# Two weight units instead of four worked tile by tile at the start of an attention, ELU and expert kernel, with a rewritten order for its first stage

## The chip, the cores and the metric

The kernel runs on one core of one Trainium2 chip. Its time is the device time of one execution in microseconds; the figure to predict is the median of several executions. TensorE is PE in the rows (PEld its weight loads), VectorE is DVE, ScalarE is ACT, GpSimd is POOL, and SyncE (SP) starts the transfers.

## What is computed

Three parts follow each other. Chunked attention over 2 x 8 heads, 768 positions, head size 64:

```python
for c in range(nc):                       # chunks of 32, with 16 before and 8 after
    k_full = concat([mem_k, k[l_start:r_end]]); v_full = concat([mem_v, v[l_start:r_end]])
    a = softmax(q_c @ k_full.T / sqrt(64))
    out[c] = a @ v_full
```

Its output is read as x with 1536 tokens of 512 columns. Then an MLP with 2048 hidden columns, and a layer of eight experts in which each token goes to the expert with the largest gate value:

```python
h = x @ w_in
g = where(h > 0, h, exp(min(h, 0)) - 1)
x = g @ w_out
# then, with capacity per expert: out[i] = gate_w[i] * (relu(x[i] @ w1[e]) @ w2[e])
```

w_in and w_out arrive as 64-bit floats and are turned into 32-bit ones on the chip, by integer operations on their words.

## The kernel before

The tokens are worked in six tiles of 256. One tile is the output of one attention pair: two blocks of 128 rows, called u = 0 and 1. The hidden columns are worked in 16 units of 128; a unit is 512 KB of w_in and 512 KB of w_out, loaded by `load_unit`.

The first stage covers tiles 0 and 1 (with attention pairs 0 and 1, and most of pair 2), and while it runs, all 16 units arrive and are converted; later tiles find them ready. Its order is written out by hand in the string `ORDER` (line 33), one word for each operation, and `do` (line 862) emits them one after the other. Each engine works its own instructions in that order, and waits where an operand or a buffer isn't there. The words are:

- `lq`, `lk`, `lv` with pair and block: loads of q, k, v; `lu` and a number: load units up to it. They stand in SP's queue in this order.
- `sc`, `tm`, `ts`, `ex`, `to`, `di`, `fl`, `fc`, `av`, `xh`, `xl` with pair and block: scores on PE (L170), the largest value and the shift on DVE (L182, L202), exponentials on ACT (L213), sums on DVE, division (L233, on POOL, or with a star on DVE), transposes on PE (L239), copy on ACT (L244), product with v on PE (L255), and the two parts (high and low) of xt, the MLP's input, on ACT (L270) and DVE (L274).
- `ca` on ACT (L358), `cb`, `cc`, `cd` on DVE (L378, L382, L391): conversion of a unit's words, 128x1024 each. `ch`, `cl` are the high and low part of the unit's w_in (L403, L407), `dh`, `dl` those of its w_out. A star moves a high part from ACT to DVE, a plus a low part from DVE to POOL.
- `ma` and a step number: the first product (`gemm1`, L454, 24 matmuls) into a PSUM bank of the pool `ph` (two banks, tile `hp`). `mr` and `mv`: ELU, three passes on ACT (L468 to L470) and two on DVE (L474, L480). `mh`, `ml`: high and low part of the ELU's output (L484, L488). `mb`: the second product (`gemm2`, L509) into the tile's two accumulators, banks of the pool `ps` (six banks, shared with the attention).
- `pw`: one matmul of the identity with itself into a `ps` bank; nothing reads it (L867). It shows as two matmul records.

A step covers two (unit, tile) halves. With `NLEAD` = 4, steps 0 and 1 are units 0 and 1, then 2 and 3, of tile 0; steps 2 and 3 the same of tile 1; from step 4 on, a step is one unit with both tiles. In the first six steps (`NWHOLE`) the second product takes w_out unsplit, as four 32-bit matmuls (eight records of 128x512); later ones take twelve. From step 16 on (`ma16`, `ma17` are the first of tile 2) a loop over the steps continues, and then the experts follow.

## Time and profile before

| | |
|---|---|
| median of 3 runs | 551.16 us (550.6 to 554.33) |
| the profiled execution | 555.13 us |
| its span, first to last instruction | 553.4 us |
| busy: PE / DVE / ACT / POOL | 523.3 / 348.1 / 293.5 / 120.1 us |
| mean granted TensorE clock | 0.976 |

The profile is one execution on the chip. [...] The timeline gives start and length of instructions, merged where they repeat, and in brackets how long the engine stood idle before them and what ended that.

### The profile page before, as it was taken

What the parts mean: (1) busy time and instruction counts of PE and PEld (TensorE: products, weight loads), DVE (VectorE), ACT (ScalarE), POOL (GpSimd) and SP (SyncE); (2) the same over time, 40 slices, a digit from 0 to 9 for tenths busy, and PEclk for the clock granted to TensorE, in tenths of its full rate; (3) what the DMA queues carried; (4) which work ended last, traced back from release to release, by engine and by line L of the source; (5) the groups of instructions that cost most, each with busy time, mean ns of one, the idle gap of its engine ahead of it and who ended that gap; (6) DMA issues with size and microseconds to landing.
All of it is one profiled execution on the core that took longest, in us unless ns stands there. A gap on an engine that the chain in (4) does not pass through costs nothing. (4 is left out here: it accounts for less than half of the span.)

```text
span 553.4 us, 11372 instructions
## 1 busy us (share of the span) xinstructions
PE 523.3 (95%) x4500; PEld 448.5 (81%) x4500; DVE 348.1 (63%) x651; ACT 293.5 (53%) x569; POOL 120.1 (22%) x108
## 2 busy tenths in 40 slices
...
GB/s 332 403 414 186 100 186 291 266 359 135 1 20 139 110 1 191 145 114 87 2 3 153 198 247 98 188 152 335 117 127 165 360 253 140 335 297 220 31 7 26
DMA packets 34725, 95.93 MB, mean 173 GB/s; under 512 B 3424, under 2 KB 3424, under 8 KB 33888
## 3 DMA queue, kind: packets, MB, share of 16 engines
...
## 5 line engine op out<-in xcount | busy, mean ns | idle before, releaser
L454 PE MATMUL hp<-xt,un 128*128 128x256 f32 x1152 | 151.1, 288 | 0.8 <-POOL un L407 0.5
L454 PEld LDWEIGHTS hp<-xt,un 128*128 128x128 f32 x1152 | 144.8, 193 | 6.6 <-issue 2.4
L509 PE MATMUL ps<-un,gt 128*128 128x512 f32 x504 | 127.2, 401 | 1.4 <-POOL gt L488 1.3
L509 PEld LDWEIGHTS ps<-un,gt 128*128 128x128 f32 x504 | 92.7, 191 | 22.5 <-POOL gt L488 2.4
L805 PE MATMUL ps<-eu,ht 128*128 128x512 f32 x336 | 84.7, 404 | 6.2 <-ACT eu L695 3.4
L696 DVE TENSOR_TENSOR eu<-eraw,eu 128x1024 fp32r<-128x1024 f32 x65 | 77.3, 1225 | 19.7 <-ACT eu L695 19.5
L805 PEld LDWEIGHTS ps<-eu,ht 128*128 128x128 f32 x336 | 62.9, 191 | 21.5 <-issue 5.7
L488 POOL TENSOR_TENSOR gt<-th,gt 128x512 fp32r<-128x512 f32 x33 | 45.8, 1388 | 127.9 <-ACT gt L484 127.8
L474 DVE SCALAR_TENSOR_TENSOR th<-e,th 128x512 f32<-128x512 f32 x48 | 34.7, 723 | 52.0 <-ACT e L470 51.8
L695 ACT CAST eu<-eraw 128x1024 fp32r<-128x1024 f32 x65 | 65.1, 1045 | 0.7 <-ACT os L811 0.7
L484 ACT CAST gt<-th 128x512 fp32r<-128x512 f32 x42 | 26.1, 620 | 73.3 <-DVE th L480 73.3
L742 PE MATMUL hp<-xd,eu 128*128 128x256 f32 x480 | 59.0, 284 | 2.9 <-DVE eu L696 2.1
L742 PEld LDWEIGHTS hp<-xd,eu 128*128 128x128 f32 x480 | 58.1, 192 | 4.3 <-DVE eu L696 2.5
...
L468 ACT ACTIVATE e<-hp 128x512 f32<-128x512 f32 x48 | 28.9, 601 | 34.2 <-PE hp L454 32.5
L811 ACT ACTIVATE os<-ps,xg 128x512 f32<-128x512 f32 x15 | 10.3, 688 | 49.1 <-PE ps L805 26.0
L407 POOL TENSOR_TENSOR un<-raw,un 128x512 fp32r<-128x512 f32 x16 | 23.6, 1481 | 56.7 <-ACT un L403 40.5
L728 DVE SCALAR_TENSOR_TENSOR ht<-hp,ht 128x512 fp32r<-128x512 f32 x20 | 13.8, 690 | 33.4 <-ACT ht L727 33.4
L469 ACT ACTIVATE th<-e 128x512 f32<-128x512 f32 x48 | 30.4, 632 | 5.9 <-DVE junk L541 3.0
L480 DVE SCALAR_TENSOR_TENSOR th<-hp,th 128x512 f32<-128x512 f32 x42 | 29.1, 692 | 4.0 <-DVE th L474 0.5
L470 ACT ACTIVATE e<-e 128x512 f32<-128x512 f32 x48 | 30.4, 632 | 1.5
L767 PE MATMUL hq<-eu,xd 128*128 128x512 f32 x120 | 30.4, 398 | 0.3 <-PE ps L805 0.3
...
## 6 DMA issues: line engine op xcount, KB each, us to landing
...
disp<-in_blank_dram SPq DMA_DIRECT2D x12, 514.0 KB, 14.9
...
```

What stands on the lines that cost most here:

```text
L454: nc.tensor.matmul(hp[:, j, :], units[f].un[:, 0, wp, kk * P : (kk + 1) * P], xts[ti][:, xp, kk, :], start=(n == 0), stop=(n == 3 * KD - 1),)
L469: nc.scalar.activation(th, e, AF.Tanh, scale=0.5)
L470: nc.scalar.activation(e, e, AF.Exp, scale=-1.0)
L474: nc.vector.scalar_tensor_tensor(out=th, in0=e, scalar=1.0, in1=th, op0=ALU.add, op1=ALU.mult)
L480: nc.vector.scalar_tensor_tensor(out=to, in0=hv, scalar=0.0, in1=th0, op0=ALU.max, op1=ALU.subtract)
L488: eng.tensor_tensor(out=gt[:, 1, :], in0=th, in1=f32(gt[:, 0, :]), op=ALU.subtract)
L509: nc.tensor.matmul(accs[ti][bl], x, w, start=(f == 0 and n == 0), stop=(f == NF - 1 and n == len(passes) - 1),)
L695: nc.scalar.copy(un[:, 0, :], raw)
L696: lows.tensor_tensor(out=un[:, 1, :], in0=raw, in1=f32(un[:, 0, :]), op=ALU.subtract)
L742: nc.tensor.matmul(hp[:, j, :], w1p(kk, wp, f * P, P), xd[xp][:, kk, :], start=(n == 0), stop=(n == 3 * KD - 1),)
L767: nc.tensor.matmul(hp, self.xd[xp][:, kk, self.b0 * P : (self.b0 + 1) * P], w1p(kk, wp, i * 512, 512), start=(n == 0), stop=(n == 3 * KD - 1),
L805: nc.tensor.matmul(acc, hof(f, gp, j), w2p(f, wp), start=(f == 0 and n == 0), stop=(f == NFE - 1 and n == 2))
```

## The change

The number of units that are worked tile by tile falls from four to two: steps 0 and 1 are units 0 and 1 of tile 0 and of tile 1, and from step 2 on a step is one unit with both tiles. There are 16 steps as before, and the first six take w_out unsplit as before. The whole string `ORDER` is rewritten. The 11 matmuls `pw` go, 20 matmuls `pm` come (8, 5 and 3 ahead of and between the first transposes, 2 before ma0, 2 before the last transposes of pair 1); they write into the bank that the next first product is going to use, so that `gemm1` takes over a bank that may already be there.

```diff
-lq00 lk00 pw pw pw pw sc00 tm00 ts00 ex00 lu0 cb0 to00 ca0 lq01 cc0 lk01 pw pw pw pw sc01
...
+lq00 lk00 pm pm pm pm pm pm pm pm sc00 tm00 ts00 ex00 to00 lk01 lq01 sc01 tm01 lu0 ca0 ts01
...
-    NLEAD, NWHOLE = 4, 6
+    NLEAD, NWHOLE = 2, 6
...
+    hps = {}
+
+    def new_hp():
+        return ph.tile([P, 2, TT], F32, tag="h", name=nm("hp"))
+
+    def idle(s):
+
+        if s not in hps:
+            hps[s] = new_hp()
+        nc.tensor.matmul(hps[s][:, 0, :], ident, ident.unsqueeze(1).to_broadcast([P, 2, P]), start=True, stop=True)
+
     def gemm1(s):
         ft = steps[s]
-        hp = ph.tile([P, 2, TT], F32, tag="h", name=nm("hp"))
+        hp = hps.pop(s, None) or new_hp()
...
+        tops = [0]
...
-            if op == "pw":
-                wp = tps([P, 2, P])
-                nc.tensor.matmul(wp, ident, ident.unsqueeze(1).to_broadcast([P, 2, P]), start=True, stop=True)
+            if op == "pm":
+                idle(tops[0])
...
                 if op == "ma":
                     pend[s] = gemm1(s)
+                    tops[0] = s + 1
```

The first place is SP's queue, from its third transfer on. Before, units are `raw_14`, `raw_24` and `raw_37`; `kt_2` and `kt_3` are the k of block 0 and 1, `v_4` and `v_5` their v, `q_1` both blocks' q:

```order
L337 DMA raw_14_161<-in_moe_w_in_dram 128x1024
L337 DMA raw_14_161<-in_moe_w_out_dram 128x1024
L141 DMA q_1_93<-in_q_dram 128x512
L141 DMA kt_3_95<-in_k_dram 128x1024
L337 DMA raw_24_221<-in_moe_w_in_dram 128x1024
L337 DMA raw_24_221<-in_moe_w_out_dram 128x1024
L141 DMA kt_2_94<-in_k_dram 128x1024
L141 DMA q_1_93<-in_q_dram 128x512
L141 DMA v_4_96<-in_v_dram 128x1024
L337 DMA raw_37_327<-in_moe_w_in_dram 128x1024
L337 DMA raw_37_327<-in_moe_w_out_dram 128x1024
L141 DMA kt_3_95<-in_k_dram 128x1024
```

In the changed kernel the units are `raw_15` and `raw_25`:

```order
L141 DMA kt_3_95<-in_k_dram 128x1024
L141 DMA q_1_93<-in_q_dram 128x512
L337 DMA raw_15_206<-in_moe_w_in_dram 128x1024
L337 DMA raw_15_206<-in_moe_w_out_dram 128x1024
L141 DMA kt_2_94<-in_k_dram 128x1024
L141 DMA q_1_93<-in_q_dram 128x512
L337 DMA raw_25_287<-in_moe_w_in_dram 128x1024
L337 DMA raw_25_287<-in_moe_w_out_dram 128x1024
L141 DMA v_4_96<-in_v_dram 128x1024
L141 DMA kt_3_95<-in_k_dram 128x1024
L141 DMA q_1_93<-in_q_dram 128x512
L141 DMA v_5_97<-in_v_dram 128x1024
```

Block 1's k and q now come ahead of unit 0, pair 1's first k and q ahead of unit 1, and unit 2, the third raw tile, falls from this place to behind both v.

The second place is PE at the start of the MLP's steps (only one of each two equal second-product rows is shown). Before, from ma1 on; `un_53` and `un_63` are units 2 and 3, `un_35` and `un_36` units 0 and 1, `xt_32` tile 0, `xt_67` tile 1:

```order
L454 MATMUL hp_76_655<-xt_32_288,un_53_454 128x256 x12
L454 MATMUL hp_76_655<-xt_32_288,un_63_550 128x256 x12
L509 MATMUL ps_78_683<-raw_14_161,gt_73_607 128x512
L509 MATMUL ps_79_684<-raw_14_161,gt_73_607 128x512
L454 MATMUL hp_84_704<-xt_67_562,un_35_323 128x256 x12
L454 MATMUL hp_84_704<-xt_67_562,un_36_325 128x256 x12
L509 MATMUL ps_78_683<-raw_37_327,gt_82_695 128x512
L509 MATMUL ps_79_684<-raw_37_327,gt_82_695 128x512
L509 MATMUL ps_91_750<-raw_14_161,gt_87_735 128x512
L509 MATMUL ps_92_751<-raw_14_161,gt_87_735 128x512
```

In the changed kernel, from mb0 on; `un_37` and `un_30` are units 0 and 1, `un_60` unit 2, `un_76` unit 3, `xt_31` tile 0, `xt_55` tile 1:

```order
L520 MATMUL ps_68_653<-raw_15_206,gt_61_623 128x512
L520 MATMUL ps_69_654<-raw_15_206,gt_61_623 128x512
L465 MATMUL hp_51_537<-xt_55_550,un_37_389 128x256 x12
L465 MATMUL hp_51_537<-xt_55_550,un_30_308 128x256 x12
L465 MATMUL hp_75_704<-xt_31_311,un_60_620 128x256 x12
L465 MATMUL hp_75_704<-xt_55_550,un_60_620 128x256 x12
L520 MATMUL ps_77_737<-raw_15_206,gt_72_696 128x512
L520 MATMUL ps_78_738<-raw_15_206,gt_72_696 128x512
L465 MATMUL hp_79_745<-xt_31_311,un_76_731 128x256 x12
L465 MATMUL hp_79_745<-xt_55_550,un_76_731 128x256 x12
```

Units 2 and 3 of tile 0, which stood ahead of mb0, are gone from there; the second step is tile 1 of units 0 and 1, and one product (unit 2, both tiles) stands between it and its own second product (`gt_72`).

The third place is DVE between unit 3's conversion and the second ELU. Before, around the first ELU, with attention rows and second rows of a pair left out; `raw_46` is unit 3 and `raw_55` unit 4:

```order
L378 TENSOR_SCALAR raw_46_393<-raw_46_393 128x1024
L382 SCALAR_TENSOR_TENSOR raw_46_393<-raw_46_393 128x1024
L228 TENSOR_SCALAR su_62_537<-su_62_537 128x8
L229 RECIPROCAL su_62_537<-su_62_537 128x8
L233 TENSOR_TENSOR a_61_536<-a_61_536,su_62_537 128x512
L391 SCALAR_TENSOR_TENSOR raw_46_393<-raw_46_393 128x1024
L403 CAST un_63_550<-raw_46_393 128x512
L474 SCALAR_TENSOR_TENSOR th_72_602<-e_71_601,th_72_602 128x512
L480 SCALAR_TENSOR_TENSOR gt_73_607<-hp_54_460,th_72_602 128x512
L378 TENSOR_SCALAR raw_55_486<-raw_55_486 128x1024
L382 SCALAR_TENSOR_TENSOR raw_55_486<-raw_55_486 128x1024
L391 SCALAR_TENSOR_TENSOR raw_55_486<-raw_55_486 128x1024
```

In the changed kernel, from the last pass of unit 2 (`raw_38`) on; `raw_54` is unit 3, `raw_63` unit 4, `raw_64` unit 5:

```order
L391 SCALAR_TENSOR_TENSOR raw_38_392<-raw_38_392 128x1024
L485 SCALAR_TENSOR_TENSOR th_45_485<-e_44_484,th_45_485 128x512
L491 SCALAR_TENSOR_TENSOR gt_61_623<-hp_6_112,th_45_485 128x512
L274 TENSOR_TENSOR xt_55_550<-ps_56_551,xt_55_550 128x2x128
L378 TENSOR_SCALAR raw_54_547<-raw_54_547 128x1024
L274 TENSOR_TENSOR xt_55_550<-ps_58_585,xt_55_550 128x2x128
L202 TENSOR_SCALAR nm_62_635<-mx_48_523 128x8
L378 TENSOR_SCALAR raw_63_637<-raw_63_637 128x1024
L382 SCALAR_TENSOR_TENSOR raw_63_637<-raw_63_637 128x1024
L378 TENSOR_SCALAR raw_64_640<-raw_64_640 128x1024
L382 SCALAR_TENSOR_TENSOR raw_54_547<-raw_54_547 128x1024
L391 SCALAR_TENSOR_TENSOR raw_54_547<-raw_54_547 128x1024
```

Unit 3 was converted ahead of the first ELU and unit 4 behind it; now only unit 2 is done by the first ELU, and units 3, 4 and 5 stand between the first and the second one.

## Rows read from the trace of the kernel before

**Rows 1.** Table of stretches: busy us (instructions) of each engine, clock, transfers.

```profile
core 0: us, PE busy (x) PEld busy (x) DVE busy (x) ACT busy (x) POOL busy (x), PEclk, DMA share, GB/s
12.00:22.00 10.00, 7.43 (x148) 5.79 (x149) 8.44 (x15) 7.88 (x27) 4.43 (x4) 0.50 1.03 415
...
32.40:39.00 6.60, 6.60 (x107) 6.45 (x101) 5.67 (x12) 3.35 (x6) 1.30 (x1) 0.50 1.03 414
36.80:126.10 89.30, 88.52 (x670) 69.92 (x669) 79.55 (x108) 60.07 (x107) 24.21 (x16) 0.99 0.73 243
```

**Rows 2.** PE's timeline to its first product: start, us, instruction, [idle before].

```profile
1.58 3.64 PE L867 MATMUL ps<-ident 128*128 128x256 f32 x8 [1.58 <-POOL ident masks.py:199]
...
6.08 1.99 PE L867 MATMUL ps<-ident 128*128 128x256 f32 x8
10.33 0.85 PE L170 MATMUL ps<-kt,q 64*32 64x64 f32 x64 [2.25 <-DMA kt<-in_k_dram]
...
14.75 1.17 PE L170 MATMUL ps<-kt,q 64*32 64x64 f32 x64 [1.16 <-DMA q<-in_q_dram]
16.75 2.13 PE L255 MATMUL ps<-at,v 64*64 64x32 f32 x64 [0.83 <-DMA v<-in_v_dram]
...
24.34 0.39 PE L454 MATMUL hp<-xt,un 128*128 128x256 f32 x1
```

**Rows 3.** PE's timeline from pair 1's last transposes to ma17.

```profile
31.01 0.63 PE L239 MATMUL ps<-ident,a 128*128 128x128 f32 x4 [1.72 <-DVE a L233]
31.57 3.47 PE L255 MATMUL ps<-at,v 64*64 64x32 f32 x128
34.97 4.93 PE L454 MATMUL hp<-xt,un 128*128 128x256 f32 x24
...
42.91 3.45 PE L454 MATMUL hp<-xt,un 128*128 128x256 f32 x24
...
80.14 2.96 PE L509 MATMUL ps<-un,gt 128*128 128x512 f32 x12
82.93 3.03 PE L454 MATMUL hp<-xt,un 128*128 128x256 f32 x24
...
93.18 2.59 PE L509 MATMUL ps<-un,gt 128*128 128x512 f32 x10 [0.65 <-POOL gt L488]
...
110.30 1.13 PE L255 MATMUL ps<-at,v 64*64 64x32 f32 x64
...
127.94 2.90 PE L454 MATMUL hp<-xt,un 128*128 128x256 f32 x22 [0.48 <-POOL un L407]
...
139.14 5.91 PE L454 MATMUL hp<-xt,un 128*128 128x256 f32 x48
```

**Rows 4.** ACT's timeline: ca0, one block's exponentials with what follows, an ELU.

```profile
8.44 1.16 ACT L358 ACTIVATE raw<-raw 128x1024 f32<-128x1024 f32 x1 [0.18 <-DMA raw<-in_moe_w_out_dram]
...
14.37 0.33 ACT L213 ACTIVATE a<-ps,nm 128x64 f32<-128x64 f32 x1
...
16.69 1.25 ACT L403 CAST un<-raw 128x512 fp32r<-128x512 f32 x2
...
32.16 0.60 ACT L468 ACTIVATE e<-hp 128x512 f32<-128x512 f32 x1
```

**Rows 5.** DVE's timeline: unit 2 landing, and a wait for an ELU.

```profile
19.16 1.13 DVE L378 TENSOR_SCALAR raw<-raw 128x1024 int32<-128x1024 int32 x1 [1.25 <-DMA raw<-in_moe_w_out_dram]
...
41.95 0.69 DVE L474 SCALAR_TENSOR_TENSOR th<-e,th 128x512 f32<-128x512 f32 x1 [1.43 <-ACT e L470]
```

**Rows 6.** Groups by form, 0 to 140 us: busy us, mean ns | idle before.

```profile
L391 DVE SCALAR_TENSOR_TENSOR raw<-raw 128x1024 int32<-128x1024 int32 x15 | 19.8, 1318 | 0.3
L382 DVE SCALAR_TENSOR_TENSOR raw<-raw 128x1024 int32<-128x1024 int32 x15 | 18.3, 1219 | 1.0 <-DVE raw L378 0.5
...
L474 DVE SCALAR_TENSOR_TENSOR th<-e,th 128x512 f32<-128x512 f32 x17 | 13.2, 779 | 8.3 <-ACT e L470 8.3
L378 DVE TENSOR_SCALAR raw<-raw 128x1024 int32<-128x1024 int32 x15 | 12.1, 820 | 2.1 <-DMA raw<-in_moe_w_out_dram 2.1
```

More of the change, by code (lines that the diff above doesn't have):

```diff
@@ L33 @@
 ORDER = """
-lq00 lk00 pw pw pw pw sc00 tm00 ts00 ex00 lu0 cb0 to00 ca0 lq01 cc0 lk01 pw pw pw pw sc01 tm01 ts01 lu1 ca1 di00 pw fl00 cd0 fc00 cb1 cc1 cd1 ex01 to01 lk10 lq10 lv00 sc10 av00 ch0 ch1 lu2 tm10 di01 cb2 lk11 xh00 xl00 ca2 pw fl01 fc01 lv01 pw av01 lq11 ts10 cl1+ cc2 cd2 lu3 ex10 lq20 to10 lk20 xh01 xl01 lv11 sc11 tm11 ts11 ch2 ca3 cb3 cc3 cl0+ ma0 lv10 lu4 sc20 lu5 lu6 di10 fl10 cl2+ ex11 to11 di11* cd3 ch3* tm20 fl11 fc10 av10 xh10* fc11 mr0 mv0 av11 xh11 xl11 lq21 cl3+ cb4 ca4 cc4 cd4 xl10 ma1 lu7 mb0 mr1 mv1 ch4 cl4+ ca6 cb6 cc6 cd6 ma2 mr2 mv2 lu8 ts20 ch6 cl6+ lk21 mb1 mb2 ma3 lu9 cb7 cb9 cb5 ca7 dh6 dl6 ex20 ca5 lu10 ca10 cc7 cd7 ca8 mr3 cc5 cd5 dh0* mv3 sc21 ma4 dl0+ to20 di20 mb3 ch5 cl5 cb8 dh1 dl1 mr4 ca9 cc9 mv4 ch7 dh2 dl2+ cb10 cl7 ma5 cd9 mr5 dh7 cc8 mv5 mb4 dh4 lu11 tm21 ca11 cd8 dl4 lu12 ca12 cc10 ma6 mr6 mv6 ch9 dh9 dh3 dl3 mh6 dl7+ mb5 dh5* lv20 cl9+ ts21 ex21 ml6+ ch8* dh8 to21 cl8+ lu13 dl8 ma7 mr7 mv7 mb6 ma8 fl20 ma9 dl5+ cb11 mh7 mr8 cd10 ch10 cb12 ml7 mb7 dl9 mv8 mh8 ml8+ mb8 cl10 ma10 cc11 cd11 mr9 mv9 lv21 lu14 dh10 dl10+ lu15 ca15 ch11 cl11 mh9 ml9 cc12 cd12 mb9 fc20 ma11 mr10 mv10 mh10 ml10 di21 mb10 fl21 ch12 dh12 cl12 ma12 dl12 cb13 dh11 dl11 ca13 cc13 cd13 mr11 mv11 ch13 cl13 fc21 mh11 ml11 ca14 cb14 cc14 av20 xh20 xl20 dh13 dl13+ mb11 cd14 ch14* mr12 dh14 mv12 mh12 ml12 cb15 cc15 av21 xh21 ma13 mr13 mv13 mh13 cl14+ ma14 xl21 mr14 dl14+ mb12 ml13 mb13 cd15 ch15* cl15+ mv14 mh14 ma15 ml14 mb14 dh15 dl15 mr15 mv15 mh15 ml15 ma16 mr16 mv16 mh16 ml16+ mb15 ma17 mr17 mv17 mh17 ml17 lw lz0 lz1 lz2 lz3 lz4 lz5 lz6 lz7 lz8 lz9 lz10 lz11
```

1 line of the change is left out of this document (added).

## The prediction

> **What bounds the kernel now.** The page gives PE 523.3 of 553.4 us, an average over stages, so I read the stretch table next. From 36.8 to 126.1 us PE is busy 88.52 of 89.3 us and DVE 79.55 [rows 1]: PE is the bound of the two-tile stage, and DVE behind it has only 9.75 us to spare. Looser is the start. [...] PE's timeline shows what it waits for at the start: 2.25 us for k of row block 1, 1.16 for a q, 0.83 for a v [rows 2], then 1.72 for a division of pair 1 on DVE [rows 3]. From 31.01 on it has two more waits, 0.65 and 0.48, until ma17 starts at 139.14 [rows 3]. [...] Behind the stage the same instructions follow in the same order and PE is full again, so I let a shift of ma17 pass to the end.
>
> **The change part by part.**
>
> *The unbroken run.* Both orders have the same products, second products and pair work. Before, ma1 begins it at 34.97; pairs 0 and 1 and ma0 are then done. In the new order the same has been done when mb0 starts, and the same work lies ahead up to ma17. Its length is 139.14 - 34.97 = 104.17, less the waits 1.13, less what ma1 lost at 1.2 GHz, 4.93 - 3.45 = 1.48 [rows 3]: 101.6 us.
>
> *When mb0 can start: transfers.* Unit 0 has landed at 8.44 (1.75 MB asked for up to there) and unit 2 at 19.16 (5.75 MB) [rows 4, 5], so 0.373 MB a us. In the new queue this puts k and q of block 1 at 7.8, unit 0 at 10.5, k and q of pair 1 at 12.5, unit 1 at 15.1, v at 16.5, the next k and q at 18.5, v at 19.8, unit 2 at 22.5, k and q of pair 2 at 25.2, v of pair 1 at 27.9, unit 3 at 30.5, unit 4 at 33.2, unit 5 at 35.9. Units 2 and 3 are no longer ahead of pair 1's second half.
>
> *Warm-ups.* The old first four took 3.64 us and the second four 1.99 [rows 2], so eight in a row end at about 7.2, and sc00 starts there and not at 5.31. That 2 us is nearly free: fl00 must wait for the division of pair 0, behind which k of pair 1 lands at 12.5 anyway; without that cover it would cost the 2 us. The other twelve stand where PE would wait, and their bank is the next product's, so they hold no attention bank.
>
> *The chain to ma0.* sc00 to 8.1; softmax of block 0 and then of block 1 on DVE to 12.4; the eight exponentials of one block take 16.69 - 14.37 = 2.3 us [rows 4], to 14.9; DVE to 16.3; ca1 (1.16 [rows 4]) has to go before the next exponentials on ACT, which end at 19.0; fc01 to 19.6; av01 with v at 19.8, 1.1 us [rows 3], to 20.9; xt's two halves to 22.8. Unit 0's last pass on DVE, its cast and its low part on POOL come out at 22.7. ma0 starts at 22.8, against 24.34 [rows 2].
>
> *From ma0 to mb0.* ma0 ends at 25.7, sc20 at 26.5. ACT ends the last exponentials of pair 1 at 26.0, then needs three passes of 0.6 [rows 4] for the ELU, to 27.9, and two copies, to 29.1. av10 and av11 end at 30.7, and mb0 takes the bank that xl10 gives up on DVE: **31.0**. Without waits ma17 then starts at 31.0 + 101.6 = 132.6, 6.5 us earlier than 139.14.
>
> *The new wait at mb1.* Step 1 is now tile 1 of the same two units, so mb1 follows ma1 by one product only. mv1 on DVE stands behind cb4, cc4, cb5, cc3, cd3 and cd4; cb5 waits 1.3 us for unit 5; mv1 is done at 41.3 and PE is ready at 40.2: 1.1 us. Behind mb1 stands ma3, and nothing else is on PE.
>
> *DVE, the cost that comes back.* At mb0 DVE has converted units 0 to 2 and one pass of unit 3; before, at that point, four units. The passes moved cost 0.82, 1.22 and 1.32 us [rows 6]. Counted with such means, DVE's list from cb4 to ch15 before is 83.6 us; the stretch shows 79.55 [rows 1], so 0.952 of it. The new list from xl11 (done at 32.3) to cl15 is 88.1 us, so 83.9: ready at 116.2 with no gap at all. To it I add the 1.3 us for unit 5 and the idle time of before that is not a wait for an ELU. Five waits for an ELU, 4.7 of the 9.75 us, the first 1.43 at 41.95 [rows 5], vanish where DVE is the late one; 5.0 stays. That gives cl15 at 122.5. PE would want it at 132.6 + 1.1 less the tail from ma15 on, two products 5.91 and three second products of 82.93 - 80.14 = 2.79 [rows 3]: 14.3, so at 119.4. ma17 therefore starts between 133.7 (PE decides) and 122.5 + 14.3 = 136.8 (DVE decides). I take 135.5, nearer to DVE's end, because before already waited 0.48 for unit 15's low part [rows 3] with 4.3 us less in the list.
>
> *At nothing.* Low parts moved between DVE and POOL: DVE gets four more and three split parts fewer, one copy of xt goes to ACT. POOL works 24.21 of 89.3 us [rows 1]. Unit 0's w_out products read the same words. If this cover is gone, one low part costs its 0.8 us on DVE.
>
> *The clock.* The first fall, before 12.0, follows the 2.25 us wait; the second, at 32.4, the 1.72 us one [rows 1 to 3]. In my chain the longest waits are about 1.2 us before fl00 and 1 us before fl01. I take PE at 2.4 GHz from sc01 on; the other end is the first rival. [...]
>
> **The sum.** 139.14 - 135.5 = 3.6 us earlier. The profiled execution took 555.13 us (span 553.4), the median is 551.16; I subtract from the median: 547.6. Bounds: 6.5 us if no new wait arises, 2.3 if DVE decides.
>
> **The rivals.**
>
> *The clock falls in the new start too.* [...] Against: the warm-ups halve the gaps. Price: three warm-ups at the rate of the first (1.2 us more), a pair of av at 3.47 instead of 2.2 [rows 3], ma0 1.48, less 0.8 us of waits that this fills: 3.2. Gain 0.4: 550.8.
>
> *DVE becomes the bound (the other side).* The place is the cl and ml parts from unit 13 on, before ma13 to ma15. If DVE keeps all its 9.75 us of idle time (each ELU still late) and the 1.3, cl15 comes at 32.3 + 83.9 + 11.05 = 127.3 and ma17 at 141.6, 2.4 us later than before: 553.6. It decides from cl15 at 124.8 on. For it: every us of DVE goes straight to the end there. Against: a late DVE finds its ELU ready.
>
> *The shift does not pass.* If the tile loop waits for something not moved, 551.2. For it only the 15% "issue" of the chain that ended last; against it the full PE behind 126.
>
> *No new wait at all.* 551.16 - 6.5 = 544.7. For it: two places with 1 to 3 us of slack in my counts; against it: both engines at over 95%.
>
> **How the numbers follow.** Chances: the forecast (545.7 to 549.2) 0.48; clock 0.18; DVE bound 0.16; not passed 0.05; no new wait 0.13. About 1% is what a measurement of this kernel can tell from no change, so the bounds are 545.6 and 556.7. Faster: the no-wait case and the forecast's near edge, 0.13 + 0.09 = 0.22. Slower: the DVE rival with DVE later by 3.1 us more, 0.05. Within 1%: 0.73. The range, 544.5 to 553.0, reaches from the no-wait case to just under the DVE rival; the likeliest case's own is 545.7 to 549.2.
>
> **What would show it.** Right: ma0 near 22.8, mb0 near 31, granted clock 1.00 from 8 to 35, a wait of about 1 us for gt at mb1, DVE over 93% busy from 36 to 120, ma17 near 135.5. Wrong: a stretch at 0.50 before 35; mb0 after 33; PE waits for un or gt behind 100 us of more than 4 us together; a stage end that has moved with a kernel end that has not.

## The result, and the profile after

The changed kernel takes 556.36 us (median of 20 executions, 552.89 to 563.9), the kernel before in the same runs 553.03 (20 executions, 548.64 to 557.09). The ratio is 1.0065, with a 95% interval of 1.0044 to 1.0086: slower by 3.6 us, where 3.6 us faster was forecast. Two executions of the changed kernel in a slower state of the chip are left out of the ratio. It lies within the 1% that had the largest chance, but outside the range: 1.0065 of the forecast's 551.16 are 554.7, and the range ended at 553.0. The profiled execution took 559.7 us, its span is 558.0.

The table of stretches of the changed kernel (length of the stretch, busy us and instructions of each engine, granted clock, DMA share, GB/s):

```profile
core 0: us, PE busy (x) PEld busy (x) DVE busy (x) ACT busy (x) POOL busy (x), PEclk, DMA share, GB/s
12.00:22.00 10.00, 5.51 (x194) 4.34 (x194) 8.89 (x15) 8.11 (x39) 2.52 (x3) 1.00 1.00 393
22.00:32.40 10.40, 8.49 (x136) 7.77 (x137) 4.59 (x13) 4.81 (x22) 5.28 (x4) 0.67 0.68 245
32.40:39.00 6.60, 4.75 (x203) 4.19 (x179) 4.80 (x8) 3.91 (x8) 1.29 (x1) 1.00 1.02 414
36.80:126.10 89.30, 83.83 (x622) 65.12 (x623) 83.58 (x107) 59.26 (x105) 24.65 (x15) 0.96 0.71 236
```

The same table of the kernel before, for the one stretch that [rows 1] leave out:

```profile
22.00:32.40 10.40, 8.29 (x276) 7.17 (x278) 9.04 (x17) 7.87 (x37) 2.32 (x2) 0.99 1.02 397
```

Before, DVE worked 9.04 and 5.67 us of the two stretches from 22.0 to 39.0; now 4.59 and 4.80. It lost 5.3 us there, and the transfers fell to 245 GB/s. From 36.8 to 126.1 the places are exchanged against [rows 1]: PE 83.83 instead of 88.52 us, DVE 83.58 instead of 79.55.

PE's timeline of the changed kernel, from the scores of pair 1's second block (L170) to ma18; L465 is the first product (L454 before), L520 the second (L509 before), L456 the warm-ups:

```profile
20.07 0.86 PE L170 MATMUL ps<-kt,q 64*32 64x64 f32 x52 [0.72 <-DMA q<-in_q_dram]
23.91 0.46 PE L170 MATMUL ps<-kt,q 64*32 64x64 f32 x12 [2.98 <-issue]
24.29 1.93 PE L255 MATMUL ps<-at,v 64*64 64x32 f32 x64
26.15 2.07 PE L456 MATMUL hp<-ident 128*128 128x256 f32 x4
27.66 4.55 PE L465 MATMUL hp<-xt,un 128*128 128x256 f32 x24
...
34.82 1.29 PE L255 MATMUL ps<-at,v 64*64 64x32 f32 x73
37.96 1.01 PE L255 MATMUL ps<-at,v 64*64 64x32 f32 x55 [1.85 <-issue]
38.91 3.86 PE L520 MATMUL ps<-raw,gt 128*128 128x512 f32 x8
...
49.37 3.86 PE L520 MATMUL ps<-raw,gt 128*128 128x512 f32 x8 [0.85 <-DVE gt L491]
...
70.98 5.48 PE L520 MATMUL ps<-raw,gt 128*128 128x512 f32 x8 [1.94 <-DVE gt L491]
...
119.09 4.60 PE L465 MATMUL hp<-xt,un 128*128 128x256 f32 x24 [1.47 <-DVE th L491]
...
144.53 5.91 PE L465 MATMUL hp<-xt,un 128*128 128x256 f32 x48
151.24 3.13 PE L465 MATMUL hp<-xt,un 128*128 128x256 f32 x24 [0.79 <-DVE th L491]
```

ma0 starts at 27.66 (forecast 22.8), mb0 at 38.91 (31.0), ma17, the second half of the line at 144.53, at 147.4 (135.5; before 139.14, [rows 3]). Two waits of the start have no releaser: 2.98 us in the middle of sc11 and 1.85 in the middle of av11. Behind the waits of 2.98, 1.94 and 1.47 us the next work runs slowly: av01 1.93 instead of the 1.14 us of av00, ma0 4.55 instead of about 2.9, mb4 5.48 instead of 3.86, ma13 4.60 instead of 3.1; the granted clock is 0.50 from 23.8, 71.6 and 119.4 us on. Behind the 1.85 us in av11 it stays at 1.00.

DVE's and POOL's timelines of the changed kernel from mb2 to mb4 (L391 a conversion pass, L485 and L491 the ELU's two passes, L407 a low part):

```profile
58.20 1.23 DVE L391 SCALAR_TENSOR_TENSOR raw<-raw 128x1024 int32<-128x1024 int32 x1
59.35 1.82 DVE L485 SCALAR_TENSOR_TENSOR th<-e,th 128x512 f32<-128x512 f32 x1
61.27 0.69 DVE L491 SCALAR_TENSOR_TENSOR gt<-hp,th 128x512 f32<-128x512 f32 x1
...
66.08 2.34 DVE L391 SCALAR_TENSOR_TENSOR raw<-raw 128x1024 int32<-128x1024 int32 x1
68.35 1.79 DVE L485 SCALAR_TENSOR_TENSOR th<-e,th 128x512 f32<-128x512 f32 x1
70.24 0.69 DVE L491 SCALAR_TENSOR_TENSOR gt<-hp,th 128x512 f32<-128x512 f32 x1
```

```profile
59.13 1.49 POOL L407 TENSOR_TENSOR un<-raw,un 128x512 fp32r<-128x512 f32 x1 [4.98 <-ACT un L403]
65.22 4.37 POOL L407 TENSOR_TENSOR un<-raw,un 128x512 fp32r<-128x512 f32 x2 [4.60 <-ACT un L403]
```

DVE never idles here, and mv4's second pass ends late for mb4. The same pass takes 0.69 us alone and 1.8 beside a POOL pass, the conversion pass 1.23 and 2.34. Added up over the DVE passes beside a POOL pass (time over the shortest of the same form) this is 11 to 12 us between 48 and 140 us, with 18 POOL passes; in the kernel before, between 36 and 128, 7 to 9 us with 17. The figure hangs a little on how much overlap is counted.

### The profile page after: what moved, and what is told of

It is laid out like the page before. It is cut to its first block, busy times and chain, and to the rows that moved or that the text cites. A ratio compares the mean times of both kernels' runs of the same rounds, so it can differ in the third digit from the quotient of the medians.

```text
span 558.0 us, 11410 instructions
## 1 busy us (share of the span) xinstructions
PE 525.0 (94%) x4518; PEld 450.8 (81%) x4518; DVE 350.4 (63%) x650; ACT 293.8 (53%) x571; POOL 119.2 (21%) x107
## 5 line engine op out<-in xcount | busy, mean ns | idle before, releaser
L465 PE MATMUL hp<-xt,un 128*128 128x256 f32 x1152 | 151.7, 289 | 2.3 <-DVE th L491 2.3
L465 PEld LDWEIGHTS hp<-xt,un 128*128 128x128 f32 x1152 | 145.5, 194 | 8.2 <-issue 4.4
L520 PE MATMUL ps<-un,gt 128*128 128x512 f32 x504 | 126.5, 400 | 0.8 <-POOL gt L499 0.6
L520 PEld LDWEIGHTS ps<-un,gt 128*128 128x128 f32 x504 | 92.8, 190 | 21.4 <-POOL gt L499 1.1
L816 PE MATMUL ps<-eu,ht 128*128 128x512 f32 x336 | 82.9, 398 | 3.2 <-ACT eu L706 2.4
L499 POOL TENSOR_TENSOR gt<-th,gt 128x512 fp32r<-128x512 f32 x36 | 50.4, 1400 | 154.0 <-ACT gt L495 153.9
L816 PEld LDWEIGHTS ps<-eu,ht 128*128 128x128 f32 x336 | 61.8, 188 | 17.7 <-issue 2.4
L485 DVE SCALAR_TENSOR_TENSOR th<-e,th 128x512 f32<-128x512 f32 x48 | 37.3, 777 | 54.2 <-ACT e L481 54.0
L407 POOL TENSOR_TENSOR un<-raw,un 128x512 fp32r<-128x512 f32 x13 | 21.2, 1637 | 51.9 <-ACT un L403 51.9
L491 DVE SCALAR_TENSOR_TENSOR th<-hp,th 128x512 f32<-128x512 f32 x42 | 29.0, 692 | 3.7
```

The source lines that it names most:

```text
L465: nc.tensor.matmul(hp[:, j, :], units[f].un[:, 0, wp, kk * P : (kk + 1) * P], xts[ti][:, xp, kk, :], start=(n == 0), stop=(n == 3 * KD - 1),)
L485: nc.vector.scalar_tensor_tensor(out=th, in0=e, scalar=1.0, in1=th, op0=ALU.add, op1=ALU.mult)
L491: nc.vector.scalar_tensor_tensor(out=to, in0=hv, scalar=0.0, in1=th0, op0=ALU.max, op1=ALU.subtract)
L499: eng.tensor_tensor(out=gt[:, 1, :], in0=th, in1=f32(gt[:, 0, :]), op=ALU.subtract)
L520: nc.tensor.matmul(accs[ti][bl], x, w, start=(f == 0 and n == 0), stop=(f == NF - 1 and n == len(passes) - 1),)
L816: nc.tensor.matmul(acc, hof(f, gp, j), w2p(f, wp), start=(f == 0 and n == 0), stop=(f == NFE - 1 and n == 2))
```

## The experiments

Four theories: **A**, the start (TensorE runs out of instructions, the clock falls, all is late); **B**, DVE's list decides from mb0 on, with **P**, POOL's help costs DVE about what it saves; **C**, the warm-ups pay; **E**, the step list. Stage lengths are read from mb1's start to mv17's second pass on DVE, which leaves the start out: 105.1 us in the changed kernel (49.37 to 154.49).

**The step list alone.** In the kernel before:

```diff
-    NLEAD, NWHOLE = 4, 6
+    NLEAD, NWHOLE = 2, 6
```

> The kernel before with the new step list alone (two units tile by tile instead of four); the order of work is that of before. Theory A (in the changed kernel TensorE runs out of instructions in its start: 2.98 us of 'issue' inside sc11 and 1.85 inside av11, the clock falls, and everything behind is late): the list costs nothing, ma17 at 139 to 140 and a time within 0.3% of before. Theory B (DVE's list between mb0 and cl15 is too long): same list as before, so also within 0.3%. Theory E (the step list itself costs, since mb1 now follows its own product at once): a wait of 1 to 3 us at mb1, repeated, and a time 2 to 4 us above before, ratio 1.004 to 1.008.

557.04 us, ratio 1.0067 (1.0038 to 1.0096). This looks like E, but PE's timeline names something else:

```profile
41.39 5.28 PE L454 MATMUL hp<-xt,un 128*128 128x256 f32 x23 [4.35 <-DVE xt L274]
```

ma1 is now tile 1's product and stands 4.35 us for xl10, which DVE makes behind unit 4's conversion, and runs slowly after it. That is the place of a word, not the list; so the list alone, with xl10 moved:

```diff
-xh11 xl11 lq21 cl3+ cb4 ca4 cc4 cd4 xl10 ma1
+xh11 xl11 xl10 lq21 cl3+ cb4 ca4 cc4 cd4 ma1
```

> The kernel before with two lead units, and with the low part of pair 1's first half (xl10) ahead of unit 4's conversion on DVE. In the run with the list alone ma1 stood 4.35 us for that part, which DVE made behind unit 4, since ma1 now takes tile 1; that wait is no property of the list. Theory B (the list is harmless, the changed kernel loses by its longer and later DVE work): ma1 waits under 0.7 us, ma17 at 138 to 140, time within 0.3% of before. Theory E (the list itself costs, by a second product right behind its first and units asked for earlier): ma17 at 142 or later, time 2 to 4 us above before.

551.89 us, ratio 1.0012 (0.9979 to 1.0045). With xl10 in its place the list costs nothing that can be measured; E falls. ma1 waited 1.07 us for it, a little more than expected.

**The place of the wait for instructions.**

```diff
-lq00 lk00 pm pm pm pm pm pm pm pm sc00
+lq00 lk00 pm pm pm pm pm pm pm pm pm pm pm pm pm pm sc00
```

> The changed kernel with six more warm-ups ahead of its first eight, which puts 12 more matmuls in front of everything. Theory A: instructions come in pieces of a fixed count, so the place of the 2.98 us wait is counted from the program's first instruction: it comes 12 matmuls earlier, after 40 of sc11's 64 matmuls instead of 52, and the 1.85 us one after about 61 of av10 and av11's 128 instead of 73. If the wait were for data of sc11, or an accident of that place, it would stay behind 52 matmuls (rival D: something on SP's queue) or vanish. Time: 0 to 3 us more than the changed kernel under every theory.

562.55 us, one execution. The wait in sc11 was not there at all; the one in av11 came after 61 matmuls, as A said:

```profile
32.03 1.12 PE L255 MATMUL ps<-at,v 64*64 64x32 f32 x61
35.30 1.80 PE L255 MATMUL ps<-at,v 64*64 64x32 f32 x67 [2.14 <-issue]
```

**The changed kernel again**, to see which of its waits belong to it:

> The changed kernel once more, nothing edited. In its first profile ma0 started at 27.66, behind 2.98 us of 'issue' inside sc11, and mb0 at 38.91; in three edited kernels whose start is nearly the same that wait was absent and ma0 started at 24.2 to 26.1. Theory A (the wait inside sc11 is part of the change's cost): it is there again, ma0 after 27. Theory B (it belonged to that one execution; DVE's list decides): no such wait, ma0 at 24.0 to 24.8, mb0 at 34.5 to 37 with the 1.5 to 2.2 us wait inside av11 still there, TensorE waits for DVE again at mb1 (0.85), mb4 (1.9), ma13 (1.5), and ma17 about 108 us behind mb0, so at 143 to 145.

560.16 us: the wait in sc11 is back with 3.31 us, the one in av11 has 2.03, mb1, mb4 and ma13 wait 0.85, 1.94 and 1.47, mb0 stands at 37.65 and ma17 at 147.8. So both profiles of this kernel have all of these waits. The one in sc11 is missing in e2, and further down in e3, e4 and e13, whose PE does the same work up to there: it comes and goes between executions.

**Less under way ahead of the instructions.**

```diff
-ch0 lv01 lu2 xl00 av01 xh01 xl01 ts11 cb2 lq21 ca2 cl0+ to10 cc2 ex11 to11 lk20 lq20 pm pm ma0 mr0
+ch0 lv01 xl00 av01 xh01 xl01 ts11 lq21 lu2 cl0+ to10 ex11 to11 lk20 lq20 pm pm ma0 cb2 ca2 cc2 mr0
```

> The changed kernel with unit 2's load moved behind the load of q that waits for sc11 (and its three conversion steps behind ma0), so that about 1 MB less is under way between 15 and 22 us. Theory A (the piece of instructions asked for at 14.8 us stands behind the loads issued before it, and came at 21.7 when they had drained): the piece comes near 19.5, the wait inside sc11 shrinks from 2.98 to under 1 us, ma0 starts at 24.5 to 25.5 instead of 27.66, the low clock near 24 us is gone or shorter, ma17 at 143 to 145 instead of 147.4, time 2 to 4 us under the changed kernel, that is within 0.3% of before. Theory B: ma0 earlier, but ma17 stays near 147 and the time that of the changed kernel (ratio to before 1.005 to 1.008). If the wait in sc11 keeps its 3 us although nothing is ahead of the piece, A's reason for the lateness is wrong.

558.22 us, ratio 1.0057 (1.0023 to 1.0090). The packet of instructions that sc11 waits for (see the next section) started at 17.7 instead of 21.6, the wait in sc11 was gone and ma0 stood at 24.65. But mb0 came at 36.68 only, behind 2.21 us in av11, and ran slowly (5.48 us); mb1 and mb4 waited 0.85 and 1.98 as before, and mv17 came at 153.93. The start was 2.7 to 3.0 us better at ma0, 0.6 to 1.0 at mb1, and the time was not: this is B's outcome, though with so little left at mb1 it is a weak test of A. It doesn't show that the later load took the wait away, since e2, e4 and e13 lacked it without that.

**DVE with less to do.** cd left out for units 6 to 13:

```diff
-            for lw, hw in zip(self.lows(), self.highs()):
+            for lw, hw in () if 6 <= self.f <= 13 else zip(self.lows(), self.highs()):
```

> The changed kernel without the conversion's last pass (the sign bits, 1.2 us on DVE each) for units 6 to 13: about 10 us of DVE's work between 49 and 120 us are left out, so it computes with wrong signs of those weights and its time is one with less work. Theory B (DVE decides from mb0 on): the waits of TensorE at mb4 (1.94), ma13 (1.47) and ma18 (0.79) and the low clock behind them (about 3 us) go, ma17 at 140 to 142 instead of 147.4, time 5 to 7 us under the changed kernel. Theory A alone (only the start matters): ma17 at 145 to 147, the two waits at the start stay at 3.0 and 1.9, time 0 to 2 us under the changed kernel.

537.87 us, ratio 0.9737 (0.9694 to 0.9779). Other signs send other tokens to other experts, so the whole time can't be compared; up to mv17 the work is the same. mb1 to mv17 took 98.0 us instead of 105.1. Of PE's waits over 0.2 us only mb1's own and ma18's are left:

```profile
45.23 3.86 PE L520 MATMUL ps<-raw,gt 128*128 128x512 f32 x8 [0.85 <-DVE gt L491]
...
140.01 3.14 PE L465 MATMUL hp<-xt,un 128*128 128x256 f32 x24 [0.79 <-DVE th L491]
```

10 us less on DVE gave 7.1: DVE decides in this stretch.

**ELU passes earlier in the list.** In the changed kernel mb4 waited 1.94 us for mv4 and ma13 1.47 for mv11, and each then ran slowly at a granted clock of 0.50 (5.48 us instead of 3.86, 4.60 instead of 3.1):

```diff
-ma5 dh2 dl2 cc9 ca7 cc7 ca11 cd9 mr4 mv4 mb4
+ma5 mr4 mv4 dh2 dl2 cc9 ca7 cc7 ca11 cd9 mb4
-fl21 fc21 cc13 cd13 ch13 dh11* dl11 ml10+ mb10 mv11
+mv11 fl21 fc21 cc13 cd13 ch13 dh11* dl11 ml10+ mb10
```

> The changed kernel with two pairs of ELU passes on DVE moved up: mv4 ahead of the conversion steps dl2, cc9, cc7, cd9, and mv11 ahead of cc13, cd13, dh11, dl11. [...] Theory B' (only the places are wrong, DVE has enough time): both waits and both slow products go, ma17 about 102 to 103 us behind mb0 instead of 107.3 to 108.5, and the time 3.5 to 6 us under the changed kernel, ratio to before 0.995 to 1.001. Theory B (the length of DVE's list decides): the waits come back at later products (mb6 to mb12, or ma14 to ma16), ma17 105 us or more behind mb0, time 0 to 2.5 us under the changed kernel.

558.18 us, ratio 1.0071 (1.0042 to 1.0100). mb4 no longer waited; mb5 did, and longer:

```profile
76.87 5.44 PE L520 MATMUL ps<-raw,gt 128*128 128x512 f32 x8 [3.36 <-DVE gt L491]
```

mb1 to mv17 took 104.9 us. A place in the list moves the wait on; its length is what costs.

Both edits (unit 2 later, ELU passes earlier):

> The changed kernel with both edits, unit 2's load behind the q that waits for sc11 and the two ELU passes earlier. Theory B': mb0 at 36 to 37 as with unit 2 later alone, ma17 102 to 103 us behind it, near 139, time at or under before (ratio 0.993 to 1.001). Theory B: ma17 105 us or more behind mb0, near 142, ratio 1.000 to 1.005.

558.17 us, ratio 1.0070 (1.0034 to 1.0107), 104.9 us from mb1 to mv17, 3.35 us at mb5: the same again.

**More work for POOL.** Nine low parts get a plus (the words alone; what stands between them is left out here and in the next two cuts):

```diff
-dl1 dl2 dl4 dl5 dl7 dl8 dl10 dl11 dl12
+dl1+ dl2+ dl4+ dl5+ dl7+ dl8+ dl10+ dl11+ dl12+
```

> The changed kernel with nine low parts of w_out (dl1, dl2, dl4, dl5, dl7, dl8, dl10, dl11, dl12; 0.8 us each on DVE) given to POOL, which works under a third of that stretch: same work, 7.2 us less on DVE. Theory B (DVE decides from mb0 on): TensorE's waits at mb4 (1.94) and ma13 (1.47) shrink to under 1 us together, ma17 comes 103 to 106 us behind mb0 instead of 108.5, and the time is 2.5 to 5 us under the changed kernel, at or below before (ratio 0.996 to 1.002). Theory A (only the start counts): ma17 still 108 us behind mb0 and a ratio of 1.004 to 1.009. If POOL becomes late in DVE's place, TensorE waits for un or gt from POOL instead.

575.17 us, ratio 1.0411 (1.0351 to 1.0471). mb4 waited 1.98 us although two of DVE's parts ahead of it were gone, and mb6 waited 13.64 us for ml6, which stands behind dl10 in POOL's order: POOL's order became the bound, as the last sentence feared, so only the unchanged mb4 says something on P.

**No help from POOL.** Fifteen low parts lose their plus:

```diff
-cl4+ dl0+ cl6+ dl3+ dl6+ cl9+ ml6+ dl9+ cl11+ ml9+ cl12+ ml10+ cl13+ ml12+ ml14+
+cl4 dl0 cl6 dl3 dl6 cl9 ml6 dl9 cl11 ml9 cl12 ml10 cl13 ml12 ml14
```

> The changed kernel with the fifteen low parts that POOL makes between mb1 and ma16 (cl4, dl0, cl6, dl3, dl6, cl9, ml6, dl9, cl11, ml9, cl12, ml10, cl13, ml12, ml14) given to DVE, 0.69 us each, 10.4 us in all. In the trace DVE's passes beside a POOL pass take up to 1.1 us longer (11.2 us in all between 48 and 140 us, of 87.7 busy). Theory P (POOL's work costs DVE about as much as doing it): the longer passes go, DVE's list grows by less than 3 us, ma17 105 to 110 us behind mb0, time within 3 us of the changed kernel. Theory B without P (DVE decides and POOL's help is real): ma17 114 us or more behind mb0, time 6 to 10 us above the changed kernel, ratio to before 1.017 or more.

569.30 us, ratio 1.0253 (1.0215 to 1.0292). Here too the order broke in one place: ml6 had been written late because POOL made it, and on DVE it stood behind all the passes ahead of it in the list, which DVE worked through without a gap from 84.9 to 97.9 us. DVE's and PE's timelines:

```profile
59.95 0.68 DVE L485 SCALAR_TENSOR_TENSOR th<-e,th 128x512 f32<-128x512 f32 x1
...
67.01 1.22 DVE L391 SCALAR_TENSOR_TENSOR raw<-raw 128x1024 int32<-128x1024 int32 x1
68.14 0.68 DVE L485 SCALAR_TENSOR_TENSOR th<-e,th 128x512 f32<-128x512 f32 x1
```

```profile
98.64 7.32 PE L520 MATMUL ps<-un,gt 128*128 128x512 f32 x22 [12.42 <-DVE gt L499]
```

Up to there P is seen plainly: the passes that took 1.82, 2.34 and 1.79 us take 0.68, 1.22 and 0.68, and mv8 comes 40.8 us behind mb1 instead of 44.8, with five more parts on DVE. The sum beside POOL fell from 11 to 12 us to 0.85.

**Only the five parts ahead of that place.**

```diff
-cl4+ dl0+ cl6+ dl3+ dl6+
+cl4 dl0 cl6 dl3 dl6
```

> The changed kernel with only the first five of POOL's low parts (cl4, dl0, cl6, dl3, dl6, between mb1 and mb5) given to DVE; everything behind keeps its place. Theory P (a POOL pass costs DVE about 1.1 us here, a low part on DVE itself 0.69): mv4 and mv5 come 1.5 to 2.5 us earlier behind mb1 than in the changed kernel (20.9 and 26.3 us), the wait at mb4 (1.94) and the slow product behind it go, mv17 101 to 103 us behind mb1 instead of 105.1, time 2 to 4 us under the changed kernel. Theory B without P: 3.4 us more work for DVE, the wait at mb4 grows to 3 us or more, time 1 to 3 us above the changed kernel.

552.90 us against 552.90 of the kernel before, ratio 1.0015 (0.9984 to 1.0046). PE's timeline at mb4:

```profile
66.33 3.87 PE L520 MATMUL ps<-raw,gt 128*128 128x512 f32 x8 [0.23 <-DVE gt L491]
69.61 3.46 PE L465 MATMUL hp<-xt,un 128*128 128x256 f32 x24
```

The wait fell from 1.94 to 0.23 us, the slow product went, mb1 to mv17 took 101.9 us. mv4 and mv5 came 19.2 and 24.9 us behind mb1, 1.7 and 1.4 earlier. DVE had 3.4 us more of its own to do, and was earlier all the same. P holds, and it is worth most of what the change lost: 3.5 us between the medians, 2.8 by the ratios.

**The warm-ups.** All 20 are taken out:

```diff
-lq00 lk00 pm pm pm pm pm pm pm pm sc00
+lq00 lk00 sc00
...
-di00 pm pm pm pm pm fl00
+di00 fl00
...
```

> The changed kernel without its 20 warm-ups (their bank goes to the product alone). [...] Theory A (they only spend instructions and push sc00 from 5 to 7.5 us): 36 matmuls fewer before ma0, so the wait of 'issue' moves from behind the 52nd matmul of sc11 to behind the 20th of av01 or goes, and the one in av11 moves behind the 109th; sc00 near 5.3, mb0 1 to 3 us earlier. Theory B: whatever the start does, mb1 still waits 0.85 and mb4 1.9 for DVE, and the time changes by less than 2 us.

560.26 us, ratio 1.0106 (1.0060 to 1.0151), so not faster. sc00 started at 5.06, ma0 at 24.62 and mb0 at 36.68, the waits for instructions moved as A said (after 19 matmuls of av01, 2.24 us; after 113 of av10 and av11, 2.12), and mv17 came at 152.76. Up to there the matmuls ran slowly: the scores took 1.17 us instead of 0.86, ma0 5.00. The start gained 1 to 2 us against the changed kernel's two profiles and mb1 none (49.75). The profile has one more wait of 2.50 us for instructions in the experts. Whether the warm-ups are worth something stays open: the difference to the changed kernel is inside the two intervals.

**Moving the pieces by 48 pairs.** Two ways were tried, and neither left the rest of the start as it was: first 32 warm-ups of 64 columns for the first eight (e14; e15 with the five parts on DVE), then 48 of a score's size for two of them (e16, with the five parts; reckoned as 46 pairs more than in e13, 552.90 us).

```diff
+            nc.tensor.matmul(hps[s][:, 0, 0:n], ident, ident[:, 0:n], start=True, stop=True)
```

```diff
+            nc.tensor.matmul(
+                hps[s][0:CH, 0, 0:n], ident[0:64, 0:CH], ident[0:64, 0:n], start=True, stop=True, tile_position=(0, 0)
+            )
```

> The changed kernel with its first eight warm-ups cut into 32 of a quarter of the width: the same columns and bank, but 48 more instruction pairs ahead of everything. Theory A (instructions come in pieces of 128 pairs of weight load and matmul; TensorE runs dry where it goes through one faster than the next one lands): the piece that began behind 73 of av10 and av11's matmuls now begins behind about 25, and the one before it at ma0's start instead of inside sc20, which gives it 6 us instead of 5; the 1.5 to 2.8 us wait inside av11 shrinks under 0.7 us or goes, and with it the slow mb0; mb0 1 to 3 us earlier, at 33.5 to 35.5. If the wait stays at the 73rd matmul of av10 and av11, the count has nothing to do with it. Time: 0 to 3 us under the changed kernel; theory B holds the gain to less than that, since mb4 still waits for DVE.

> Both edits. If the two causes are those of the miss, they add: mb0 at 33.5 to 35.5, no wait over 1 us behind mb1 but ma13's, ma17 at 138 to 141 (before: 139.1; changed kernel: 147.4 and 147.8), and a time of 5 to 7 us under the changed kernel, ratio to before 0.995 to 1.001. If the time does not follow ma17, the rest lies behind 155 us.

> [...] Theory A: the piece that began behind 73 of av10 and av11's 128 matmuls begins behind about 29; asked for at ma0's start and not inside sc20, it lands in time, the 1.95 us wait goes, mb0 at 33.5 to 34.5 instead of 35.97 and the time 1 to 2 us under the same kernel without it. Against A: the wait moves to about the 29th matmul and keeps its 1.5 to 2.5 us; time within 1 us.

561.57, 558.25 and 563.49 us, ratios 1.0176 (1.0136 to 1.0217), 1.0121 (1.0085 to 1.0156) and 1.0197 (1.0160 to 1.0234). PE's first line in e14 and in e16, and the wait in av10 and av11 of e14 and of e16:

```profile
1.58 13.92 PE L457 MATMUL hp<-ident 128*128 128x64 f32 x64 [1.58 <-POOL ident masks.py:199]
```

```profile
1.58 10.44 PE L457 MATMUL hp<-ident 64*32 64x64 f32 x96 [1.58 <-POOL ident masks.py:199]
```

```profile
39.44 0.59 PE L255 MATMUL ps<-at,v 64*64 64x32 f32 x25
42.50 1.72 PE L255 MATMUL ps<-at,v 64*64 64x32 f32 x103 [2.47 <-issue]
```

```profile
45.89 0.54 PE L255 MATMUL ps<-at,v 64*64 64x32 f32 x19 [1.68 <-issue]
```

A quarter of the columns took more than half the time (0.22 us a record against 0.39), and the small matmuls into one place 0.11 us a record, two records each, not the 0.012 of a score; so the first scores came 7.7 to 9.2 us late and none of the three shows what the wait is worth. They show its place: e14's stands after 25 matmuls, where A put it (e15 had none there), and e16's, with 92 records more in front and not the 46 reckoned, after 109. And they repeat e13: with the five parts the same start is 3.3 us faster (561.57 to 558.25), though e15's profile also lacks the wait in av10 that e14's has, so not all of it need be theirs.

**What helped, together.** Five parts on DVE, unit 2 later, mv11 earlier:

> The changed kernel with five of POOL's low parts on DVE, unit 2's load behind the q that waits for sc11, and mv11 ahead of cc13, cd13, dh11 and dl11. Each took a wait away where it was tried (2.98 inside sc11, 1.47 at ma13). Theory B with P (DVE decides, POOL lengthens it): DVE has 0 to 2 us to spare now, so ma13's wait shrinks to 0.5 to 1 and the time is 0 to 2 us under the kernel with five parts alone, ratio to before 0.997 to 1.002. If only the start counted (A), 2 us or more less: 0.995 to 0.998.

554.00 us, ratio 1.0028 (0.9998 to 1.0057): no gain over the five parts alone. ma13 waited 0.95 us for POOL's cl13 instead, and the wait in sc11 was there (1.98) in spite of the later load, so the load's place is not what decides it.

**Does a shift pass to the end?** In the kernel before, 22 matmuls of the warm-ups' form stand in ma17's bank ahead of ma17, so that TensorE alone works longer there; 9.5 us were reckoned, about what the changed kernel's mv17 is late, and its profile shows 9.66:

```diff
+        for _ in range(22 if s == 17 else 0):
+            nc.tensor.matmul(hp[:, 0, :], ident, ident.unsqueeze(1).to_broadcast([P, 2, P]), start=True, stop=True)
```

> [...] If a shift there passes to the end as the forecast let it: time 8.5 to 10 us above before, ratio 1.015 to 1.018. If later stages give part of it back: 3 to 6 us, ratio 1.005 to 1.011, and the changed kernel's 3.3 us are what is left of its 9.5.

```profile
137.28 9.66 PE L451 MATMUL hp<-ident 128*128 128x256 f32 x44
```

557.15 us, ratio 1.0092 (1.0058 to 1.0126): 3.2 to 7.0 us of the 9.5 arrive. The kernel before a second time, with nothing edited:

> The kernel before once more, nothing edited. Its first profile had ma1 at 34.97, ma17 at 139.14, and in the experts two stretches about 2.6 us longer each than in the other profiles. Every theory: ma1 at 34.5 to 37 (later by up to 2 us where TensorE runs out of instructions inside av11, for which its first profile had 0.5 us to spare), ma17 at 139 to 141; from the tenth split of the experts (405.25) to the end 143 to 149 us.

557.70 us: ma1 at 35.42, behind 0.31 us of waiting for instructions in av11, mv17 at 144.78 (144.96 in the first profile), the end 149.2 us behind the place in the experts that stood at 405.25 in the first profile (148.2 there). From mv17 to the end of the span the two profiles of before take 408.5 and 411.2 us; the changed kernel 403.5 twice, the five parts 400.6, e18 401.0. PE's waits over 0.6 us behind 390 us add up to 8.1 us in the first profile of before, with the clock at 0.50 for 3.4 us from 513.5 on; in the changed kernel's they are 6.7 us, and the clock doesn't fall before the last 4 us. The two largest of before (2.18 and 2.21 in its second profile), which the changed kernel's profile has not at these places:

```profile
446.76 5.83 PE L805 MATMUL ps<-eu,ht 128*128 128x512 f32 x24 [3.23 <-ACT eu L695]
...
512.96 5.77 PE L805 MATMUL ps<-eu,ht 128*128 128x512 f32 x17 [1.91 <-issue]
```

That does not show that a late kernel gets its delay back there. Both profiles of before are of executions longer than its median (555.13 and 557.70 us against 553.0), and e7 does not have the first of these waits, although its PE comes to the product ahead of it within 0.2 us of e6's. PE's timelines of e6 and of e7 there:

```profile
447.27 5.04 PE L805 MATMUL ps<-eu,ht 128*128 128x512 f32 x14 [2.18 <-ACT eu L695]
```

```profile
445.15 5.74 PE L805 MATMUL ps<-eu,ht 128*128 128x512 f32 x24
```

So e18's times show that part of a delay is lost on the way to the end; at which place was not found.

## Why the prediction was wrong

**The unbroken run of 101.6 us and the step list: right.** With its waits taken off, the stage takes what was reckoned: in e13 ma17 comes at 141.3, 105.3 us behind mb0, with waits of 3.7 us in it (0.86, 0.23, 0.78, 0.34 and 1.48); and the list alone moves nothing that can be measured (1.0012).

**"With v at 19.8, 1.1 us, to 20.9 ... ma0 starts at 22.8", mb0 "31.0": wrong, the larger part of the delay at ma17 (7.9 of 11.9 us).** The chain counted data, engines and transfers, and took the supply of instructions as free. In the profile mb0 is 7.9 us late: 2.98 in sc11, 1.85 in av11, and the slow av01, warm-ups and ma0 behind the first (0.8, 1.0 and 1.65), together 8.3. Where the first wait was missing or under 0.3 us (e3, e4, e9, e12, e13) ma0 stood at 22.67 to 24.65, close to the forecast, and mb0 at 34.76 to 37.62, still 4 to 7 us late. Part of that is the wait in av11 (1.73 to 2.77 us, none in e12), part a second error of the chain, in its transfers: it let them follow each other at 0.373 MB a us without a gap, and had k and q of pair 2 there at 25.2. But SP's next load behind unit 2 is a q that takes over the buffer from which sc11 reads, and SP stood until sc11 was done: from 15.2 to 24.46 in the changed kernel's profile, whence the 245 GB/s, and from 14.6 to 21.5 in e13, where sc20 then waited 1.61 us. SP's and PE's timelines of e13:

```profile
14.18 0.45 SPq L337 DMA_DIRECT2D raw<-in_moe_w_out_dram  x1
21.50 0.33 SPq L141 DMA_DIRECT2D q<-in_q_dram  x1
```

```profile
29.12 0.85 PE L170 MATMUL ps<-kt,q 64*32 64x64 f32 x64 [1.61 <-DMA q<-in_q_dram]
```

In e9, e12 and e17 the same wait is 1.12, 3.01 and 2.03 us; in the changed kernel's own profiles PE is later than the q. The supply of instructions shows in the page of the changed kernel as a queue:

```profile
q8 instruction: 46, 0.75, 0.6%
```

0.75 MB in 46 packets are 16.3 KB each. Counted from PE's first matmul, the waits stand behind matmul 347 or 348, 475, 601 and 729 in every run that has them, whatever is computed there: 126 to 128 matmuls with their weight loads, about 254 instructions. In the changed kernel's two PE goes on 1.37 and 1.22 us behind the end of one of the packets (ends at 22.54 and 36.74), in the other runs' waits over 1 us 1.2 to 1.5. That PE waits for these packets is read from the counts and the times; the trace names no releaser. At number 601, in the changed order inside av11, the wait goes with the time that PE took for the 128 matmuls ahead: 3.7 to 3.9 us in eleven runs of that order, with waits of 1.7 to 2.8; 4.9 us in e1, e7 and e18, with 0.75 to 1.47; 5.5 to 6.8 us in both profiles of before, e12, e15 and e16, with 0 to 0.31. Only e14 took 7.1 and still waited 2.47, behind a packet that came late. So the kernel before was near the same edge.

One piece ahead of the wait in sc11, PE passes its count of 220 near 14.6 us, inside sc10; the next packet started at 21.6 in the profile, when the loads issued up to 15.2 us were nearly through, and at 17.7 in e3. But it started at 17.4 in e4 too, with the same loads; why it is late in some executions only stays open.

**"I take PE at 2.4 GHz from sc01 on": wrong.** No run shows a clock in GHz, neither the 2.4 here nor the 1.2 at which the sum has ma1 lose 1.48 us; the profile shows granted clocks of 1.00 and 0.50, and before, ma1 took 4.93 us with 0.50 up to 39.1 us, a product of the same form at 1.00 took 3.45. In the changed kernel the clock was 1.00 up to 23.8 and then 0.50 for 6.8 us, behind the wait in sc11 (stretch 22.0 to 32.4: 0.67). The rival with the low clock priced the fall at 3.2 us; the wait ahead of it here was in none of the cases. But e3 and e4, without that wait, fell to 0.50 as well, from 19.9 and 19.1 us on, behind waits of 0.9 to 1.7 us for divisions and a q, as the two falls of the kernel before did, while e13, with waits of the same size, kept 1.00 to 546 us. What makes the difference stays open.

**"Nearly free" warm-ups: open**, see e11.

**The new wait at mb1, 1.1 us: the size right, the mechanism not; that was luck.** The wait is 0.85 or 0.86 us in every run of this order but e15 (2.38). The forecast had mv1 late on DVE, behind the conversions and 1.3 us of waiting for unit 5. In the profile DVE is through with those passes and stands idle for ACT:

```profile
47.83 0.69 DVE L485 SCALAR_TENSOR_TENSOR th<-e,th 128x512 f32<-128x512 f32 x1 [1.51 <-ACT e L481]
```

What PE waits for is the length of the ELU itself, from 45.7 us (its first pass on ACT) to 49.3 (mv1's second pass), while PE has one product to do. Only e15 had DVE wait for unit 5 (0.82 us) and work without a gap from there to mv1. **DVE over 93% busy from 36 to 120: right**: 83.58 of 89.3 are 93.6%.

**"0.952 of it", and low parts between DVE and POOL "at nothing": wrong, and the one step whose repair moved the time.** The list was scaled by what the kernel before showed, where POOL's passes cost DVE 7 to 9 us; in the new order they cost 11 to 12. The difference lies between mb1 and mb5, where DVE had nothing to spare: 5 to 6 us there, against 1.3 to 2.1 in the kernel before and 2 in e13. The forecast looked for DVE's end at cl15 and ma15; it showed earlier, as ELU passes that stand behind conversions, at mb4 (1.94) and ma13 (1.47), each with 1.5 to 1.7 us of slow product behind it, which no term had. From mb0 to ma17 this made 108.5 us instead of 104.5. What makes a pass longer no run shows; the rows show which passes: L485 reads e and th, both in SBUF, and takes 0.69 alone and up to 1.82 beside POOL; L378 reads one input, in SBUF, and takes 0.68 alone and 1.79 and 1.81 beside POOL; L491 reads one of its inputs from PSUM and stays at 0.69, in four passes beside POOL as in the rest. The rival "DVE becomes the bound" (553.6, ma17 at 141.6) was the nearest case: the right engine, at another place than cl15 and with its price too low.

**"I let a shift of ma17 pass to the end": wrong.** e18 passes 3.2 to 7.0 of 9.5 us. The changed kernel's mv17 is 9.5 us late between the first profiles (144.96 to 154.49) and its time 3.6, but the two can't be set against each other as they stand: its profiled execution took 559.7 us, 3.3 more than its median. Whether a gain at ma17 would pass in full no run shows. (The forecast's upper edge, 549.2, doesn't follow from its bound of 2.3 us either, which gives 548.9; nothing hangs on that.)
